# RWKV-6 with a channel MLP on one core: w, k and r of rounds 3 to 7 turned by VectorE from runs of steps, and the first level taken from loads one step back

## The chip, the cores and the metric

One core of a Trainium2 chip. The time is that of one execution on the device, in microseconds; the figure of a kernel is the median of its runs. Shares of busy time and single instructions come from one profiled execution.

## The reference

The first block is a linear recurrence over 768 steps, for 4 batches and 8 heads of 48 channels; the second a normalization and a two-layer MLP with a residual.

```python
for t in range(S):
    cur = einsum('bhd,bhe->bhde', u[None] * kt, vt)
    y[:, :, t] = einsum('bhd,bhde->bhe', rt, state + cur)
    state = wt[:, :, :, None] * state + einsum('bhd,bhe->bhde', kt, vt)
...
x = y.transpose(0, 2, 1, 3).reshape(B, S, H * D)
xn = (x - mu) / np.sqrt(var + 1e-06) * g_ln
out = x + np.maximum(xn @ w_ch1, 0.0) @ w_ch2        # 384 -> 1536 -> 384
```

Everything is float32.

## The kernel before, in words

**Units, rounds and levels.** The work is cut into eight rounds, numbered from 0, one for each batch and half of the sequence (384 steps). A round has two units of four heads. In a unit the 384 steps are six chunks of 64 steps, for each of two pairs of heads. Inside a chunk the weights from step s to step t (r at t times the decays between times k at s) are built in six levels: at level 0 for steps one apart, at level 1 for blocks of 2, and so on to blocks of 32. At each level PE multiplies k and r of all chunks (`quads`, result `a_ps`), then VectorE multiplies the later half of each block of r and of k by the block's decay product (`grow`, tile `rkT`), and copies the level's blocks under a mask into the matrix A (`keep`; at level 0 it is an AND with `bits`). PE needs the grown `rkT` for the next level.

**What feeds a round.** w, k and r of the next round are loaded with the steps on the partitions (`load`, tiles `nat_w`, `nat_k`, `nat_r`, one of each for an even and an odd unit), three transfers of 128 steps for each tensor and unit. PE turns them to channels on the partitions with an identity (`turned`: three transposes of 128x128 to a PSUM tile `w_ps`, `k_ps` or `r_ps`), and ScalarE copies them to SBUF: 36 transposes and 12 copies a round. This is done while the round before runs, at its levels 1 (w of both units), 2 (k and r of the first) and 3 (of the second); in round 2 at levels 3, 4 and 5. GpSimd (POOL) builds the products of decays over blocks (`totals`, tile `tot`, the last one `decay`). The term of the step itself, r times u times k summed over channels, comes from the untransposed tiles: `own_products` on POOL (tile `rk`), `own_sums` on VectorE (tile `own`), and times v in `own_term` on POOL (tile `vo`).

**What ends a round.** At levels 0 and 1 of the next round `states` runs for the two units of the old one (PE's `kv`, then ten dependent steps on VectorE, tile `s`), at levels 2 and 3 `outputs` (PE's `y`, to which VectorE adds `vo`, tile `x`). At level 5 `ends` turns k back (`kn_ps`).

**The MLP.** The MLP of a finished round is a list of 24 steps of three matmuls each (twelve for `h_ps`, twelve for `o_ps`). `fill(until, tasks)` puts them between the tasks of a level, so that PE has work while VectorE grows the next level; the table `UNTIL` says how many steps lie behind each level. From round 4 on it is four steps a level, in round 3 three. The tasks of a level are spread evenly over its MLP steps. A float32 matmul is two instructions on PE, so three matmuls read as x6 in the trace.

**Order.** PE, ScalarE, VectorE and POOL run in the order in which the program is written (`InOrder`, lines 39 to 48). Nearly all transfers are issued by SP, one queue in order: behind a transfer that waits for a buffer all later ones wait. The pool `p4` has four buffers a tag; its tag `raw` holds raw MLP weights early in the program. Every call goes through one helper, so that line 49 stands for all of them and the tiles tell them apart.

Lines: `load` 122, `turned` 306, `totals` 340, `own_products` 358, `own_sums` 369, `own_term` 401, `quads` 411, `grow` 431, `keep` 448, `states` 504, `outputs` 560, `mlp` 635, `fill` 692, the loop over rounds and levels from 821.

Of the kernel before, what the change touches and what calls it, by code (L numbers as in the profile page):

```python
# [9 lines left out]
F32 = mybir.dt.float32  # L10
# [42 lines left out]
def kernel(  # L53
# [79 lines left out]
    def load_rows(nm, q, eng):  # L133

        b, f, g = units[q]
        src = {"w": w, "k": k, "r": r}[nm]
        eng.dma_start(
            out=flat(nm, q)[:, 0 : NH * TT * D].rearrange("p (h x) -> p h x", h=NH),
            in_=src[b, ts(g, NH), ds(f * RN, RN)].rearrange("h (p c) d -> p h (c d)", c=TT),
        )  # L140

    def load_v(q, eng=SP):
# [161 lines left out]
    st, carry = {}, {}  # L304

    def turned(q, nm, pr):
        a = st.setdefault(q, {})
        if pr == 0:
            if nm == "w":
                if q % U == 0:  # L310
                    st["w"] = p1.tile([P, U, W], F32, tag="w", name=f"wT{q // U}")
                a["w"] = st["w"][:, q % U]
            elif "rk" not in a:

                rk = a["rk"] = p4.tile([P, 2, W], F32, tag="rkT", name=f"rkT{q}")
                a["r"], a["k"] = rk[:, 0], rk[:, 1]
        ps = ps_t.tile([P, RN], F32, tag="t", name=f"{nm}_ps{q}_{pr}")
# [40 lines left out]
    def own_products(q, eng):  # L358
        b, f, g = units[q]
        rk = st[q]["ruk"] = p1.tile([P, TT, NH, D], F32, tag="rk", name=f"rk{q}")  # L360
        eng.tensor_tensor(
            out=rk, in0=nat["k"][q % 2][..., 0:D], in1=nat["r"][q % 2][..., 0:D], op=ALU.mult
        )
        eng.tensor_tensor(
            out=rk, in0=rk,
            in1=u_bc[:, ts(g, NH)][:, None].broadcast_to([P, TT, NH, D]), op=ALU.mult,
        )

    def own_sums(q):
        o = st[q]["own"] = p4.tile([P, TT, NH], F32, tag="own", name=f"own{q}")  # L370
        DVE.tensor_reduce(out=o, in_=st[q]["ruk"], axis=AX.X, op=ALU.add)

    def products(q, eng=DVE):
# [27 lines left out]
    def own_term(q, eng):  # L401
        a = st[q]
        a["vo"] = p4.tile([P, TT, NH, D], F32, tag="vo", name=f"vo{q}")
        eng.tensor_tensor(
            out=a["vo"], in0=vn[q],
            in1=a["own"][:, :, :, None].broadcast_to([P, TT, NH, D]), op=ALU.mult,
        )

    a_ps = {}
# [38 lines left out]
    def keep(rnd, lev):  # L448
        n = 1 << lev
        A, ps = a_bufs[rnd % 2], a_ps[rnd]  # L450
        if lev == NLEV - 1:
# [268 lines left out]
    def units_of(rnd):  # L720
        return [U * rnd + g for g in range(U)] if rnd < NR else []

    def take(eng, q):

# [96 lines left out]
    for rnd in range(1, NR + 1):  # L821
# [3 lines left out]
        for lev in range(NLEV):  # L825
            slot = (rnd - 1) * NLEV + lev
            if rnd == 2:

                for q in old if lev < 2 else []:
                    (states, outputs)[lev](q)  # L830
                if lev < 2:
                    mlp_step()
            elif old and lev < 2 * U:
# [3 lines left out]
            for q in now:  # L837
                if slot:
                    quads(q, lev)
# [8 lines left out]
            if rnd == 1:  # L848
# [10 lines left out]
                if lev == 3:  # L859
                    tasks += each(load_vx, now, [SPO])  # L860
                if lev == 1:
                    tasks += each(product_sums, now)
                if lev in (4, 5):
                    own_term(now[lev - 4], POOL)
            if rnd == 2 and lev == 0:
                tasks += each(load_v, now) + each(load, new, "w")
            if rnd == 2 and lev == 2:
# [3 lines left out]
            if rnd == 2 and lev in (3, 4):  # L871
                tasks += each(own_term, now[lev - 3 :][:1], [POOL])
            if rnd > 2 and lev < 2:
                tasks += each(load, new, ["w", "kr"][lev])
            first = 3 if rnd == 2 else 1
            if rnd > 1 and new and first <= lev < first + 3:
                m = lev - first
                tasks += each(turned, new[m - 1 : m], "kr", pairs) if m else each(
                    turned, new, "w", pairs
                )  # L880
            if rnd == 2:
# [8 lines left out]
            if lev == 3 and rnd > 1:  # L890
                for q in now:
                    load_vx(q)
                for q in new:
                    load_v(q)
                if rnd > 2:
                    moments(rnd - 1)
                    tasks += each(norm, [rnd - 1])
            if lev == 4 and rnd > 2:
                tasks += each(turned_x, [rnd - 1], range(KC))
                tasks += each(own_products, new[:1], [POOL])  # L900
            if lev == NLEV - 1:

                if now:
                    mlp_step()
                if rnd > 2 and new:
                    own_sums(new[0])
                if rnd == 2:
                    tasks += each(own_products, new[:1], [POOL]) + each(own_sums, new[:1])
                if rnd >= 2:
                    tasks += each(own_term, new[:1], [POOL])  # L910
                    tasks += each(own_products, new[1:], [POOL])
                    tasks += each(own_sums, new[1:]) + each(own_term, new[1:], [POOL])
# [9 lines left out]
            if rnd == 1 and lev < NLEV - 1:  # L922

                n = (1, 2, 2, 1, 0, 0)[lev] * NP
                tasks += mixed([begin] * BEGINS[lev], [join] * JOINS[lev], ahead[:n])
                del ahead[:n]
# [35 lines left out]
```

## Time and profile before

| | |
|---|---|
| median of 11 runs | 586.73 us (584.99 to 590.91) |
| the profiled execution | 589.29 us, of it 587.5 from the first instruction to the last |
| PE busy | 574.9 us |
| VectorE (DVE) busy | 272.2 us |
| ScalarE (ACT) busy | 194.0 us |
| GpSimd (POOL) busy | 91.7 us |
| mean granted clock of TensorE | 0.985 |
| bytes moved | 36.52 MB, 62 GB/s |

A row of a timeline has the start, the length, the engine, the operation with out<-in, and, in brackets, how long the engine sat idle before it and what released it. A row of a group has the count, the busy time and the mean of one in ns, then the idle time before. For PE the mean of one overlaps with the next, so what PE steps cost is read from the start of one row to the start of another.

### The profile page before, as it was taken

The page shows a single profiled execution, that of the slowest core. Times are in us where ns is not written, and L with a number is a line of the kernel's source. Part 1 is how long each engine was busy: PE and PEld are TensorE (multiplying, and loading weights), DVE is VectorE, ACT ScalarE, POOL GpSimd, SP SyncE. Part 2 cuts the span into 40 slices and gives each one's busy share as a digit, 9 for nine tenths or more (in the row PEclk, how much of TensorE's full clock was granted, in tenths as well). Part 3 has the DMA queues.
Part 4 walks back from the last instruction along what each step waited for, and adds up shares of the span by engine and source line. Part 5 has one row for each costly group of instructions (what it writes and reads, how often), then busy time and mean ns, then how long its engine had stood idle before and what let it go on. Part 6 is the DMA issues. An engine that isn't in the chain of part 4 may idle for free.

```text
span 587.5 us, 19053 instructions
## 1 busy us (share of the span) xinstructions
PE 574.9 (98%) x8558; PEld 385.9 (66%) x8558; DVE 272.2 (46%) x576; ACT 194.0 (33%) x423; POOL 91.7 (16%) x124
## 2 busy tenths in 40 slices
PE   8999999999999999999999999999999999999997
PEld 6876765666666666676666666666666665666554
DVE  5788888777255443434362443336244441130000
ACT  3567597402452225212423115412241015202200
POOL 6130010204250026000530008000330000000000
PEclk9789799999999999999999999999999999999999
DMA  9938696046214402340204302021000000000000
GB/s 230 207 95 161 151 239 153 2 92 134 52 36 81 91 16 41 63 87 25 56 3 87 71 29 42 1 53 40 15 2 2 16 28 2 2 15 27 0 15 27
DMA packets 114192, 36.52 MB, mean 62 GB/s; under 512 B 104768, under 2 KB 111040, under 8 KB 114112
## 3 DMA queue, kind: packets, MB, share of 16 engines
q1 hardware_dynamic: 112240, 34.72, 26.8%
q8 instruction: 67, 1.10, 0.8%
q10 hardware_dynamic: 1872, 0.59, 0.4%
q14 instruction: 13, 0.11, 0.1%
HBM read 28.51 MB, written 4.72 MB: 57 GB/s over the span
## 4 chain that ended last, share of the span: by engine, by line
PE 92%; DVE 3%; ACT 3%; issue 1%; DMA 1%; ACTq 0%; DVEq 0%
PE o_ps L49 32%; PE h_ps L49 31%; PE a_ps L49 12%; PE y L49 4%; PE k_ps L49 2%; PE kv L49 2%; PE r_ps L49 2%; PE w_ps L49 2%; PE kn_ps L49 2%; PE xT_ps L49 1%; DVE w_sb L49 1%; PE own_ps L49 1%; PE idle L49 1%; ACT rest L49 1%; DVE rkT L49 1%
## 5 line engine op out<-in xcount | busy, mean ns | idle before, releaser
L49 PE MATMUL o_ps<-w_sb,h 128*128 128x384 f32 x576 | 199.1, 490 | 1.0 <-ACT h L49 1.0
L49 PE MATMUL h_ps<-xT,w_sb 128*128 128x384 f32 x576 | 199.6, 494 | 0.0
L49 PEld LDWEIGHTS h_ps<-xT,w_sb 128*128 128x128 f32 x576 | 106.0, 192 | 63.3 <-issue 1.2
L49 PEld LDWEIGHTS o_ps<-w_sb,h 128*128 128x128 f32 x576 | 104.3, 190 | 62.4 <-ACT h L49 2.3
L49 DVE TENSOR_TENSOR rkT<-rkT,tot 128x768 f32<-128x768 f32 (+1 forms) x96 | 75.7, 829 | 41.9 <-issue 26.0
L49 ACT ACTIVATE h<-h_ps 128x384 f32<-128x384 f32 x96 | 46.9, 489 | 145.0 <-PE h_ps L49 144.9
L49 PEld LDWEIGHTS a_ps<-rkT 48*64 48x64 f32 x4608 | 74.0, 138 | 21.0 <-issue 14.0
L49 PE MATMUL a_ps<-rkT 48*64 48x32 f32 x4608 | 79.2, 222 | 0.1
L49 DVE TENSOR_TENSOR o<-o_ps,x 128x384 f32<-128x384 f32 x24 | 13.4, 556 | 121.9 <-PE o_ps L49 121.8
L49 POOL TENSOR_TENSOR vo<-v,own 128x576 f32<-128x576 f32 x16 | 19.0, 1190 | 289.8 <-DVE own L49 250.2
L49 DVE SCALAR_TENSOR_TENSOR s<-s,decay,kv 128x48 f32<-128x48 f32 x160 | 29.3, 257 | 33.9 <-PE kv L49 33.9
L49 DVE TENSOR_TENSOR x<-y,vo 128x288 f32<-128x288 f32 x32 | 13.1, 452 | 54.5 <-PE y L49 54.5
L49 DVE COPY_PREDICATED A<-mask,a_ps 128x768 f32<-128x768 int8 x32 | 38.3, 1196 | 0.0
L49 ACT COPY rkT<-k_ps 128x384 f32<-128x384 f32 x31 | 13.9, 478 | 57.3 <-PE k_ps L49 57.1
L49 ACT ACTIVATE xT<-xT_ps,g_sb 128x384 f32<-128x384 f32 x24 | 13.6, 580 | 54.0 <-PE xT_ps L49 54.0
L49 ACT COPY rkT<-r_ps 128x384 f32<-128x384 f32 x31 | 14.2, 478 | 25.9 <-PE r_ps L49 25.9
L49 DVE TENSOR_SCALAR w_sb<-w_sb 128x384 f32<-128x384 f32 (+1 forms) x48 | 19.4, 405 | 0.8
L49 PE MATMUL r_ps<-ident,nat_r 128*128 128x128 f32 x108 | 16.7, 285 | 2.4 <-ACT rkT L49 1.6
L49 ACT COPY wT<-w_ps 128x384 f32<-128x384 f32 x31 | 13.9, 478 | 14.5 <-PE w_ps L49 14.4
L49 ACT ACTIVATE rstd<-mv,eps 128x3 f32<-128x3 f32 x8 | 2.4, 296 | 49.2 <-DVE mv L49 49.1
L49 DVE TENSOR_REDUCE own<-rk 128x12 f32<-128x576 f32 x12 | 9.0, 750 | 20.7 <-POOL rk L49 20.6
L49 PEld LDWEIGHTS r_ps<-ident,nat_r 128*128 128x128 f32 x108 | 13.0, 142 | 8.0 <-issue 2.5
(76 smaller groups left out, 524.5 us busy)
## 6 DMA issues: line engine op xcount, KB each, us to landing
raw<-in_moe_w_ch_dram SPq DMA_DIRECT2D x24, 384.0 KB, 4.1
v<-in_v_dram SPq DMA_DIRECT2D x48, 96.0 KB, 3.1
out_dram<-o SPq DMA_DIRECT2D x24, 192.0 KB, 1.9
nat_w<-in_w_dram SPq DMA_DIRECT2D x42, 96.0 KB, 3.1
nat_r<-in_r_dram SPq DMA_DIRECT2D x42, 96.0 KB, 2.8
nat_k<-in_k_dram SPq DMA_DIRECT2D x42, 96.0 KB, 2.9
vx<-v SPq DMA_DIRECT2D x28, 72.0 KB, 2.4
nat_r<-in_r_dram ACTq DMA_DIRECT2D x2, 288.0 KB, 5.0
```

The source lines that it names most:

```text
L49: return lambda *args, **kw: self.tc.keep_in_program_order(f(*args, **kw))
```

## The change

**Turning.** From round 3 on (prepared in rounds 2 to 6) w, k and r are no longer turned by PE. For each unit, tensor and pair of heads `stage` loads a tile in which a partition holds 12 consecutive steps of one head, and `squares` turns it by one VectorE instruction of 12 squares of 32x32 into channels on partitions, in place of three PE transposes and a ScalarE copy. A square needs 32 channels at a time, so a head takes two groups of 32 partitions, the second shifted by 32 channels and reading into the next step beyond channel 48. A tile is thus four transfers of 32 partitions by 560 numbers (2240 bytes each, one run in memory), and a round has 48 of them. The tiles use the four `raw` buffers. Staging of a level's tiles is issued one level before their squares: the staging of k and r of the first unit waits for the squares of w, that of the second unit for those of the first.

**The first level.** From round 3 on `quads` and `keep` leave level 0 out. Its entries of A are set to zero once in each of the two A buffers. Instead k and v are loaded a second time, one step back (`load_before`, into the `nat_w` tiles, which are free now), and the own term gets a second part: r times the k of the step before, summed over channels, kept at odd steps only (`next`), times the v of the step before. This is one more POOL step in `own_products`, a reduction and a small multiplication in `own_sums`, and two more POOL steps in `own_term`. k and r are still loaded with steps on partitions for these products. `grow` at level 0 stays. The two units of a round share the tiles one step back, so the second unit's load waits for the first unit's use.

**PE, levels 0 and 1 of round 4.** Before, from the states of an old unit at level 0 to the middle of level 1:

```order
L49 MATMUL kv_3310<-v_2259,kn_3244 64x48 x24
L49 MATMUL a_ps_0_3345<-rkT_2906 64x32 x24
L49 MATMUL a_ps_0_3345<-rkT_3058 64x32 x24
L49 MATMUL h_ps_0_4_3397<-xT_3150,w_sb 128x384 x3
L49 MATMUL h_ps_0_5_3406<-xT_3150,w_sb 128x384 x3
L49 MATMUL h_ps_0_6_3415<-xT_3150,w_sb 128x384 x3
L49 MATMUL h_ps_0_7_3424<-xT_3150,w_sb 128x384 x3
L49 MATMUL kv_3431<-v_2263,kn_3266 64x48 x24
L49 MATMUL a_ps_1_3466<-rkT_2906 64x32 x24
L49 MATMUL a_ps_1_3466<-rkT_3058 64x32 x24
L49 MATMUL h_ps_0_8_3527<-xT_3150,w_sb 128x384 x3
L49 MATMUL w_ps_0_3537<-ident,nat_w_88 128x128 x3
```

The same place on PE now:

```order
L49 MATMUL kv_3323<-v_2275,kn_3246 64x48 x24
L49 MATMUL h_ps_0_4_3371<-xT_3145,w_sb 128x384 x3
L49 MATMUL h_ps_0_5_3382<-xT_3145,w_sb 128x384 x3
L49 MATMUL h_ps_0_6_3393<-xT_3145,w_sb 128x384 x3
L49 MATMUL h_ps_0_7_3402<-xT_3145,w_sb 128x384 x3
L49 MATMUL kv_3409<-v_2279,kn_3270 64x48 x24
L49 MATMUL a_ps_1_3444<-rkT_2907 64x32 x24
L49 MATMUL a_ps_1_3444<-rkT_3078 64x32 x24
L49 MATMUL h_ps_0_8_3510<-xT_3145,w_sb 128x384 x3
L49 MATMUL h_ps_0_9_3519<-xT_3145,w_sb 128x384 x3
```

The level-0 products and the transposes are gone; MLP steps follow one another.

**VectorE, from level 5 to level 1 of the next round.** Before, from the two own sums of the coming round's units on (the second waits for POOL), then the old unit's states, level 0 and its mask, the other unit's states, level 1:

```order
L49 TENSOR_REDUCE own_4038<-rk_3968 128x12
L49 TENSOR_REDUCE own_4068<-rk_4053 128x12
L49 COPY s_4105<-kv_4106 128x48 x2
L49 SCALAR_TENSOR_TENSOR s_4105<-s_4105,decay_3297,kv_4106 128x48 x10
L49 TENSOR_TENSOR rkT_3686<-rkT_3686,wT_3536 128x2x384
L49 TENSOR_TENSOR rkT_3848<-rkT_3848,wT_3536 128x2x384
L49 TENSOR_TENSOR A_125<-a_ps_0_4143,bits_163 128x768
```

The same place on VectorE now:

```order
L49 TENSOR_REDUCE own_4015<-rk_3944 128x12
L49 TENSOR_REDUCE next_4017<-nat_w_88 128x12
L49 TENSOR_SCALAR next_4017<-next_4017,odd 128x12
L49 TENSOR_REDUCE own_4062<-rk_4053 128x12
L49 TENSOR_REDUCE next_4064<-nat_w_88 128x12
L49 TENSOR_SCALAR next_4064<-next_4064,odd 128x12
L49 COPY s_4099<-kv_4100 128x48 x2
L49 SCALAR_TENSOR_TENSOR s_4099<-s_4099,decay_3310,kv_4100 128x48 x10
L49 TENSOR_TENSOR rkT_3668<-rkT_3668,wT_3508 128x2x384
L49 TENSOR_TENSOR rkT_3849<-rkT_3849,wT_3508 128x2x384
```

The sums one step back stand before the states, and the masking of level 0 is gone. Four squares (`STREAM_TRANSPOSE`) follow the masks of levels 1 and 2 and the normalization at level 3.

**SP, around level 2.** Before, from the loads of the coming units' k, r and w on:

```order
L125 DMA nat_k_91<-in_k_dram 128x4x48 x3
L125 DMA nat_r_93<-in_r_dram 128x4x48 x3
L125 DMA nat_w_88<-in_w_dram 128x4x48 x3
L125 DMA nat_w_89<-in_w_dram 128x4x48 x3
L145 DMA v_4624<-in_v_dram 128x4x48 x3
```

SP now, after the loads of w's runs:

```order
L125 DMA nat_k_91<-in_k_dram 128x4x48 x3
L125 DMA nat_r_93<-in_r_dram 128x4x48 x3
L163 DMA k_runs_0_3525<-in_k_dram 32x560 x4
L163 DMA k_runs_1_3530<-in_k_dram 32x560 x4
L163 DMA r_runs_0_3535<-in_r_dram 32x560 x4
L163 DMA r_runs_1_3546<-in_r_dram 32x560 x4
L163 DMA k_runs_0_3676<-in_k_dram 32x560 x4
L163 DMA k_runs_1_3681<-in_k_dram 32x560 x4
L163 DMA r_runs_0_3689<-in_r_dram 32x560 x4
L163 DMA r_runs_1_3694<-in_r_dram 32x560 x4
L743 DMA out_dram<-o_0_0_3702 128x384
```

Thirty-two transfers of runs stand between the loads of k and r and the first output; each group of four waits for VectorE's squares to free its buffer.

**The diff**, cut to its core; `FIRST` is 3:

```diff
+    def stage(q, nm, pr, eng=SP):
...
+        t = p4.tile([P, WC, 2], F32, tag="raw", name=f"{nm}_runs{q}_{pr}")
+        t = staged[q, nm, pr] = t.rearrange("p n two -> p (n two)")[:, 0 : NS * D]
+        for j in range(2):
+            first = src.offset + ((b * H + g * NH + 2 * pr + j) * S + f * RN) * D
+            for e in range(HP // SQ):
...
+                eng.dma_start(
+                    out=t[ds(HP * j + SQ * e, SQ), 0:n],
+                    in_=bass.AP(
+                        tensor=src.tensor, offset=first + SQ * e, ap=[[NS * D, SQ], [1, n]]
+                    ),
+                )
+    def load_before(q, src, i, eng=SP):
...
+        for c in range(TT):
+            eng.dma_start(
+                out=nat["w"][i][:, c, :, 0:D],
...
+    def squares(q, nm, pr):
+        a = st[q] if pr else turned_to(q, nm)
+        DVE.transpose(
+            out=a[nm][:, ts(pr, RN)].rearrange("p (t s) -> p s t", s=NS),
+            in_=staged.pop((q, nm, pr)).rearrange("p (s d) -> p s d", s=NS)[..., 0:SQ],
+        )
@@ own_products
+        if q >= FIRST * U:
+            k1 = nat["w"][0][..., 0:D]
+            eng.tensor_tensor(out=k1, in0=k1, in1=nat["r"][q % 2][..., 0:D], op=ALU.mult)
@@ own_sums
+            DVE.tensor_reduce(out=o, in_=nat["w"][0][..., 0:D], axis=AX.X, op=ALU.add)
+            DVE.tensor_scalar(out=o, in0=o, scalar1=odd, scalar2=None, op0=ALU.mult)
@@ own_term
+            eng.tensor_tensor(out=a["vo"], in0=a["vo"], in1=v1, op=ALU.add)
@@ loop over rounds and levels
             for q in now:
-                if slot:
+                if slot and (lev or rnd < FIRST):
                     quads(q, lev)
...
-            if rnd > 1 and new and first <= lev < first + 3:
+            if rnd > 1 and new and first - 1 <= lev < first + 3:
                 m = lev - first
-                tasks += each(turned, new[m - 1 : m], "kr", pairs) if m else each(
-                    turned, new, "w", pairs
-                )
+                turns = [(new, "w"), (new[:1], "kr"), (new[1:], "kr")]
+                if m >= 0:
+                    tasks += each(squares, *turns[m], pairs)
+                if m < 2:
+                    tasks += each(stage, *turns[m + 1], pairs)
...
-                    tasks += each(norm, [rnd - 1])
+                    tasks = each(norm, [rnd - 1]) + tasks
...
                 if rnd >= 2:
+                    tasks += each(load_before, new[1:], [k], [0])
                     tasks += each(own_term, new[:1], [POOL])
+                    tasks += each(load_before, new[1:], [v], [1])
                     tasks += each(own_products, new[1:], [POOL])
```

Two smaller edits come with it: the own sums of round 1 on PE are mixed among the other tasks of their level, and round 2 places an MLP step between the outputs of its two old units as well as behind them.

85 lines of the change are left out of this document (64 added, 21 removed).

## Prediction

> **What bounds the kernel now.** I read the page's busy times first, then the chain that ended last, then busy times by stretch over the rounds that the change touches.
>
> ```profile
> span 587.5 us, 19053 instructions
> PE 574.9 (98%) x8558; PEld 385.9 (66%) x8558; DVE 272.2 (46%) x576; ACT 194.0 (33%) x423; POOL 91.7 (16%) x124
> PE 92%; DVE 3%; ACT 3%; issue 1%; DMA 1%; ACTq 0%; DVEq 0%
> 145.00:213.00 68.00, 66.75 (x1135) 45.70 (x1127) 31.98 (x64) 22.23 (x50) 12.09 (x12) 1.00 0.31 61
> 213.00:281.00 68.00, 68.00 (x1073) 45.75 (x1073) 27.77 (x58) 19.77 (x44) 12.80 (x12) 1.00 0.24 50
> 281.00:349.00 68.00, 68.00 (x1069) 45.83 (x1069) 28.42 (x63) 19.76 (x44) 13.20 (x12) 1.00 0.24 50
> 349.00:417.00 68.00, 68.00 (x1093) 45.84 (x1087) 27.94 (x59) 19.76 (x44) 12.96 (x12) 1.00 0.15 33
> ```
>
> The stretches give length, then busy time of PE, PE's weight loads, DVE, ACT and POOL, then clock, DMA share and GB/s. From 213 to 417 us PE never pauses, at full clock, while DVE is busy 28 of 68 us. PE time that goes there shortens the run one for one, unless another engine makes PE wait. So I need two things: what PE steps are worth from start to start, and how much room each new DVE step has before PE's next use of it.
>
> **What it removes from PE.** Times are read from start to start, since matmuls overlap and their busy times count the overlap twice. This is round 5 on PE, from level 0 (first three rows) to the end of level 1.
>
> ```profile
> 292.42 1.57 PE L49 MATMUL a_ps<-rkT 48*64 48x32 f32 x96
> 293.92 8.01 PE L49 MATMUL h_ps<-xT,w_sb 128*128 128x384 f32 x24
> 301.86 0.92 PE L49 MATMUL kv<-v,kn 64*64 64x48 f32 x48
> ...
> 304.09 2.20 PE L49 MATMUL h_ps<-xT,w_sb 128*128 128x384 f32 x6
> 306.13 0.49 PE L49 MATMUL w_ps<-ident,nat_w 128*128 128x128 f32 x3
> ...
> 308.39 0.82 PE L49 MATMUL w_ps<-ident,nat_w 128*128 128x128 f32 x6
> ...
> 310.99 0.49 PE L49 MATMUL w_ps<-ident,nat_w 128*128 128x128 f32 x3
> ...
> 313.35 0.25 PE L49 MATMUL y<-v,A 64*64 64x48 f32 x1
> ```
>
> The first-level products take 293.92 - 292.42 = 1.50 us. Four MLP steps alone take 301.86 - 293.92 = 7.94 us; four MLP steps with 12 transposes take 313.35 - 304.09 = 9.26 us, so 12 transposes are worth 1.32 us, 0.11 us each. A round has 36 of them, 3.95 us.
>
> - Transposes of five rounds: 5 x 3.95 = 19.8 us.
> - First-level products of rounds 3 to 7: 5 x 1.50 = 7.5 us.
>
> A regular round shrinks by 5.45 us. The Trainium skill (TensorE: Matmul & The Clock Gate, Part 4) gives a PE transpose about 275 ns in a kernel and 390 ns alone; by 275 ns the 180 transposes would be 49 us and the gain about 57 us, an estimate. The step of 0.11 us decides here: the latency shows only in the duration of one, not in the queue's advance.
>
> With the transposes goes a small wait for their PSUM copies in round 2:
>
> ```profile
> 158.32 0.55 PE L49 MATMUL k_ps<-ident,nat_k 128*128 128x128 f32 x3 [0.58 <-ACT rkT L49]
> 159.44 0.93 PE L49 MATMUL r_ps<-ident,nat_r 128*128 128x128 f32 x6 [0.19 <-ACT rkT L49]
> 160.55 0.55 PE L49 MATMUL kn_ps<-ident,rkT 128*128 128x128 f32 x3 [0.18 <-ACT rkT L49]
> ```
>
> That is 0.95 us. ACT also loses twelve copies a round, and is on no chain here.
>
> **What it adds to DVE: squares.** No 32x32 transpose stands in the trace. The nearest rows of 384 elements a lane or more:
>
> ```profile
> L49 DVE TENSOR_TENSOR o<-o_ps,x 128x384 f32<-128x384 f32 x24 | 13.4, 556 | 121.9 <-PE o_ps L49 121.8
> L49 DVE COPY_PREDICATED A<-mask,a_ps 128x768 f32<-128x768 int8 x32 | 38.3, 1196 | 0.0
> L49 POOL TENSOR_TENSOR vo<-v,own 128x576 f32<-128x576 f32 x16 | 19.0, 1190 | 289.8 <-DVE own L49 250.2
> ```
>
> I take 0.56 us (same size, one pass), with 1.2 us as the upper end and 0.4 below. Twelve a round are 6.7 us, plus two more reductions, less the 0.95 us masking of level 0: DVE goes from 28 of 67.8 us to about 36 of 62.4. What matters is where they stand:
>
> ```profile
> 178.39 1.87 DVE L49 COPY_PREDICATED A<-mask,a_ps 128x768 f32<-128x768 int8 x1
> 214.12 1.20 DVE L49 TENSOR_TENSOR rkT<-rkT,tot 128x384 f32<-128x384 f32 x2 [0.36 <-PE a_ps L49]
> 306.58 1.86 DVE L49 COPY_PREDICATED A<-mask,a_ps 128x768 f32<-128x768 int8 x1
> 335.64 1.26 DVE L49 TENSOR_SCALAR xn<-x,mv,rstd 128x384 f32<-128x384 f32 x3
> 349.74 2.14 DVE L49 TENSOR_TENSOR rkT<-rkT,tot 128x384 f32<-128x384 f32 x4 [0.36 <-PE a_ps L49]
> ```
>
> The tightest level is 3: xn ends at 336.90, and by 349.74 DVE owes level 4's two multiplications (1.83), its mask (about 1) and an output addition (0.56). With 1.32 us of PE time gone from between, 12.84 - 1.32 - 3.4 = 8.1 us is left for four squares: they cost nothing up to 2.0 us each. In round 3, whose levels are shorter, the room is some 4 us, 1.0 us each. Cover is thus there at 0.56; at 1.2 only round 3 pays, about 1 us.
>
> **What it adds to SP: the staging.** Per round 48 transfers of 32 rows replace six for w; six loads one step back come on top, k and r's own loads stay.
>
> ```profile
> 308.70 4.06 SPq L125 DMA_DIRECT2D nat_w<-in_w_dram  x6
> nat_w<-in_w_dram SPq DMA_DIRECT2D x42, 96.0 KB, 3.1
> L49 SPq DMA_DIRECT2D raw<-in_moe_w_ch_dram x24: 327/340/1241, 4.5 to 91.9; - x24
> ```
>
> A level's batch is 16 transfers. At raw's issue of 0.34 us and a landing of 3.1 us a batch takes 16 x 0.34 + 3.1 = 8.5 us; at nat_w's 0.68 us apiece, 14.0 us. I take 8.5: a transfer has 32 rows, and raw's 128 rows are the nearer. The four buffers make batch, squares, batch, squares a chain on DVE and SP: from the mask of level 1 to the multiplications of level 5 are 349.74 - 308.44 = 41.3 us, less 3.95 that PE saves, less 3.4, less two times four squares (4.5): 29.4, or 14.7 us a batch. In round 3 it is 214.12 - 180.26 = 33.9, so 11.0 us a batch. Both hold 8.5; at 14.0 round 3 alone pays 6 us. Batch w goes out a level ahead, with no squares before it.
>
> **What it adds between rounds.** Level 5 of round 5, level 0 of round 6; T counts from level 5's products on PE.
>
> ```profile
> 348.72 1.60 PE L49 MATMUL a_ps<-rkT 48*64 48x32 f32 x96
> 359.50 0.92 PE L49 MATMUL kv<-v,kn 64*64 64x48 f32 x48
> 351.80 0.75 DVE L49 TENSOR_REDUCE own<-rk 128x12 f32<-128x576 f32 x1
> 356.67 0.75 DVE L49 TENSOR_REDUCE own<-rk 128x12 f32<-128x576 f32 x1 [4.12 <-POOL rk L49]
> 360.49 1.84 DVE L49 SCALAR_TENSOR_TENSOR s<-s,decay,kv 128x48 f32<-128x48 f32 x10 [3.06 <-PE kv L49]
> 355.22 1.41 POOL L49 TENSOR_TENSOR rk<-rk,u_bc 128x576 f32<-128x576 f32 x1
> 358.61 1.47 POOL L49 TENSOR_TENSOR tot<-wT 128x768 f32<-128x768 f32 x1
> 362.25 1.82 DVE L49 TENSOR_TENSOR rkT<-rkT,wT 128x768 f32<-128x768 f32 x2
> 355.17 1.49 SPq L125 DMA_DIRECT2D nat_k<-in_k_dram  x3
> ```
>
> DVE's second own sum already waits 4.12 us for POOL, and queued behind it are the states and level 0's multiplications. New order: own sum ends T = 3.8, next sum and its mask of odd steps 4.7; POOL own term 1.2 + 1.2 + 1.4, ending 7.6; the second unit's products 3 x 1.45, ending 11.9; DVE's next sum to 12.8, states 1.84, multiplications 1.82, ending 16.5. PE wants these for level 1 at 10.8 + 0.7 + 7.9 + 0.7 = 20.2, since no level 0 stands before it now: 3.7 us of room. Two-input steps of DVE and POOL can hold each other:
>
> ```profile
> 168.21 3.39 DVE L49 TENSOR_TENSOR rkT<-rkT,wT 128x768 f32<-128x768 f32 x2
> 168.79 2.00 POOL L49 TENSOR_TENSOR rk<-rk,u_bc 128x576 f32<-128x576 f32 x1
> ```
>
> Here two multiplications took 3.39 instead of 1.82, so 2.1 us is left. The second unit's load one step back starts after the first unit's next sum, T = 4.7, issues for 1.5, lands 3.1 later, 9.3; POOL wants it at 10.5. The decay totals start at 15.5, first one done at 17.0; DVE wants it at about 22. All hidden. In round 2 the last squares fall into this very level, 2.2 us and a wait for their batch of perhaps 2, against 2.1 to 3.7: 0 to 2 us late. With round 3's shorter levels I take 2 us of new waits, bounds 0 and 10.
>
> **The sum.** The profiled run took 589.29 us (span 587.5). 589.3 - 19.8 - 7.5 - 0.95 + 2.0 = 563.0. That run lies 2.56 us above the median of 586.73; the median goes to 586.7 - 26.2 = **560.5 us**, own range 557 to 565.
>
> **The rivals.** (a) The level boundary becomes late: POOL's longer chain, the load in it and port conflicts eat the 2.1 us and 2 us more, every round. For it: 4.12 us of waiting there today, and three more POOL steps a unit. Against: 3.7 us of room by durations. Price 5 x 2 = 10 us: 570.5.
>
> (b) Slower: the staging is the bound. Place: levels 1 to 3, SP and the four buffers. It decides where a batch passes 14.7 us; each microsecond more costs PE 2 a round, and at 17.4 us, about 0.9 us a transfer beyond the landing, the 5.45 us are gone. With 1.0 us each a batch is 19.1, 2 x 4.4 = 8.8 us a round, and 44 us over five: 604.5. For it: nat_w's 0.68 us apiece with larger transfers. Against: nat_w's transfers go out 0.68 us apart in sixes and still land after a median of 3.1 us; one after another the sixth would land after 6 x 3.1 - 3.4 = 15. They overlap. The Trainium skill (DMA: Bandwidth & Descriptors, Rules for kernel authors) advises against splitting a load over parts of the partitions, since the parts serialize, and puts some 2.0 us of fixed cost on a DMA; by that a batch would be 32 us, an estimate. The row's landings disagree with that reading.
>
> (c) The squares are slow, 2 us or more each: level 3 fills, and each 0.1 us above costs 0.4 us a round. At 2.4 us that is 8 us in the regular rounds and more in round 3: 573. Nothing but the absence of a row is for it.
>
> (d) That PE waits elsewhere and nothing is gained is excluded by the three stretches with PE busy 68.00 of 68.00.
>
> **How the numbers follow.** Forecast 0.66; (a) 0.20; (b) 0.05; (c) 0.04; better than 557, through shorter tails behind small matmuls, 0.05. The range 556.5 to 573 leaves out (b), part of (a) and (c), and a little below. A difference under 0.3% (1.8 us) cannot be told from none. Faster 0.92 (all but (b) and the tails of (a) and (c)), same 0.02, slower 0.06.
>
> **What would show it.** Right: PE still without pauses from 213 us on; a regular round of about 62.4 us instead of 67.8; squares near 0.56 us; staging landed before its squares on DVE; level 0's multiplications done before PE's level 1. Wrong: PE idle before a_ps released by DVE, growing each round ((a) if at level 1, (b) or (c) if at levels 4 and 5); DVE idle before a square, released by a DMA (b).

## The result, and the profile after

The changed kernel takes **565.74 us** (median of 12 runs, 563.67 to 568.25) where the kernel before takes 586.95 us beside it: ratio 0.9639, 95% interval 0.9619 to 0.9658. That is 21.2 us faster; the forecast was 26.2 us faster, 560.5 us. The profiled execution of the changed kernel took 565.91 us. One run of an experiment, `r2_early`, took 1107.25 us in a slower state and is left out of that kernel's figures.

First the page: span, busy times, and the chain that ended last by engine.

```profile
span 564.2 us, 18202 instructions
PE 547.8 (97%) x7898; PEld 359.2 (64%) x7898; DVE 333.1 (59%) x654; ACT 168.9 (30%) x363; POOL 133.7 (24%) x157
PE 82%; DVE 7%; ACT 4%; SPq 2%; issue 2%; DMA 1%; POOL 1%; DVEq 0%; POOLq 0%; ACTq 0%
```

PE is busy 27.1 us less (574.9 before), while its pauses grew from 587.5 - 574.9 = 12.6 to 16.4 us. Its share of the chain fell from 92% to 82%. Where the pauses are, the stretches show (length, busy time of PE, its weight loads, DVE, ACT and POOL, then clock, DMA share, GB/s):

```profile
145.00:205.00 60.00, 55.58 (x889) 35.91 (x888) 46.91 (x87) 13.38 (x29) 19.57 (x18) 0.97 0.64 146
205.00:270.00 65.00, 65.00 (x949) 41.91 (x949) 41.33 (x77) 14.74 (x32) 22.34 (x19) 1.00 0.53 118
270.00:330.00 60.00, 60.00 (x910) 39.42 (x911) 40.83 (x77) 14.75 (x32) 21.35 (x18) 1.00 0.56 126
330.00:395.00 65.00, 65.00 (x941) 41.83 (x939) 40.32 (x73) 14.75 (x32) 21.07 (x21) 1.00 0.53 117
```

From 205 to 395 us PE never pauses. The loss is in round 2 and its boundary to round 3, where the first staged round is prepared. PE's waits there, with the pause and what ended it in brackets:

```profile
137.57 4.14 PE L49 MATMUL h_ps<-xT,w_sb 128*128 128x384 f32 x12 [1.36 <-DVE o L49]
...
149.17 1.60 PE L49 MATMUL a_ps<-rkT 48*64 48x32 f32 x96
...
153.60 0.88 PE L49 MATMUL kn_ps<-ident,rkT 128*128 128x128 f32 x6 [0.69 <-DVE rkT L49]
...
169.76 0.90 PE L49 MATMUL a_ps<-rkT 48*64 48x32 f32 x48 [2.28 <-DVE rkT L49]
171.81 1.05 PE L49 MATMUL a_ps<-rkT 48*64 48x32 f32 x48 [1.15 <-DVE rkT L49]
172.79 7.56 PE L49 MATMUL o_ps<-w_sb,h 128*128 128x384 f32 x18
```

The row at 149.17 has no wait; it is the products of level 5, from which the boundary is counted. All waits but the first end with DVE's `rkT`, so the question goes to DVE, then to POOL and SP, for which DVE waited:

```profile
149.32 0.86 DVE L49 STREAM_TRANSPOSE rkT<-k_runs 128x384 f32<-128x384 f32 x1 [1.13 <-DMA k_runs<-in_k_dram]
150.48 0.86 DVE L49 STREAM_TRANSPOSE rkT<-r_runs 128x384 f32<-128x384 f32 x1 [0.30 <-DMA r_runs<-in_r_dram]
152.30 0.85 DVE L49 STREAM_TRANSPOSE rkT<-r_runs 128x384 f32<-128x384 f32 x1 [0.96 <-DMA r_runs<-in_r_dram]
...
161.00 0.87 DVE L49 STREAM_TRANSPOSE rkT<-r_runs 128x384 f32<-128x384 f32 x1 [2.00 <-DMA r_runs<-in_r_dram]
...
164.98 0.75 DVE L49 TENSOR_REDUCE next<-nat_w 128x12 f32<-128x576 f32 x1 [1.71 <-POOL nat_w L49]
...
167.99 3.77 DVE L49 TENSOR_TENSOR rkT<-rkT,wT 128x768 f32<-128x768 f32 x2
```

```profile
155.67 1.15 POOL L49 TENSOR_TENSOR vo<-v,own 128x576 f32<-128x576 f32 x1 [11.81 <-DVE own L49]
...
163.54 1.41 POOL L49 TENSOR_TENSOR nat_w<-nat_w,nat_r 128x576 f32<-128x576 f32 x1 [1.05 <-DMA nat_w<-in_k_dram]
```

```profile
150.78 3.62 SPq L163 DMA_DIRECT2D k_runs<-in_k_dram  x8
154.50 4.96 SPq L163 DMA_DIRECT2D r_runs<-in_r_dram  x8
159.55 1.50 SPq L174 DMA_DIRECT2D nat_w<-in_k_dram  x3
```

DVE waits 4.39 us for staged runs. It does so ahead of the first unit's own sums too, and POOL, which waits for these, starts its chain late. On SP the second unit's load one step back stands behind the last batch and goes out only at 159.55; POOL waits 1.05 us for it, DVE's `next` waits for POOL, and level 0's multiplications end at 171.76, after PE has run out of work.

A regular boundary, round 4 to 5, for comparison (DVE, POOL, PE):

```profile
280.57 0.75 DVE L49 TENSOR_REDUCE own<-rk 128x12 f32<-128x576 f32 x1 [5.61 <-POOL rk L49]
...
284.97 3.77 DVE L49 TENSOR_TENSOR rkT<-rkT,wT 128x768 f32<-128x768 f32 x2
```

```profile
273.78 1.15 POOL L49 TENSOR_TENSOR vo<-v,own 128x576 f32<-128x576 f32 x1 [6.06 <-DVE own L49]
```

```profile
269.88 1.60 PE L49 MATMUL a_ps<-rkT 48*64 48x32 f32 x96
...
290.18 1.57 PE L49 MATMUL a_ps<-rkT 48*64 48x32 f32 x96
...
332.45 1.60 PE L49 MATMUL a_ps<-rkT 48*64 48x32 f32 x96
```

The multiplications end at 288.74, the second unit's last. PE takes the first unit's at 290.18 and the second's one half (0.75 us) later, so the room is 290.93 - 288.74 = 2.2 us.

Counted from level 5's products on PE, level 0's multiplications begin after 284.97 - 269.88 = 15.1 us here and after 167.99 - 149.17 = 18.8 at the end of round 2, 3.7 later. Of that, 2.6 us are there when POOL begins the first unit's own term (after 3.9 us here, 6.5 there), and 1.05 is the wait for the load one step back. PE on its side is done with its other work after 20.3 us here and after 18.3 there (169.76 - 2.28 - 149.17). 2.2 - 3.7 - 2.0 = -3.5 us: these are PE's waits of 2.28 and 1.15.

The regular round lasts 332.45 - 269.88 = 62.57 us.

The squares, as a group and at level 3 of the same round:

```profile
L49 DVE STREAM_TRANSPOSE rkT<-r_runs 128x384 f32<-128x384 f32 x20 | 15.6, 837 | 3.3 <-DMA r_runs<-in_r_dram 3.3
259.00 1.54 DVE L49 STREAM_TRANSPOSE rkT<-k_runs 128x384 f32<-128x384 f32 x2
...
262.23 1.79 DVE L49 TENSOR_TENSOR rkT<-rkT,tot 128x768 f32<-128x768 f32 x2
```

One takes 0.84 us alone and 15.6 / 20 = 0.78 us in line; level 4's multiplications end at 264.02, 5.9 us ahead of PE's products at 269.88.

### The profile page after: what moved, and what is told of

Same layout as the page of the kernel before. It is cut to its first block, busy times and chain, and to the rows that moved or that the text cites. A ratio compares the mean times of both kernels' runs of the same rounds, so it can differ in the third digit from the quotient of the medians.

```text
span 564.2 us, 18202 instructions
## 1 busy us (share of the span) xinstructions
PE 547.8 (97%) x7898; PEld 359.2 (64%) x7898; DVE 333.1 (59%) x654; ACT 168.9 (30%) x363; POOL 133.7 (24%) x157
## 4 chain that ended last, share of the span: by engine, by line
PE 82%; DVE 7%; ACT 4%; SPq 2%; issue 2%; DMA 1%; POOL 1%; DVEq 0%; POOLq 0%; ACTq 0%
PE o_ps L49 33%; PE h_ps L49 27%; PE a_ps L49 9%; PE y L49 4%; PE kv L49 2%; DVE rkT L49 2%; DVE w_sb L49 2%; ACT rest L49 2%; PE kn_ps L49 2%; SPq L163 1%; PE xT_ps L49 1%; PE own_ps L49 1%; PE k_ps L49 1%; PE idle L49 1%; PE r_ps L49 1%
## 5 line engine op out<-in xcount | busy, mean ns | idle before, releaser
L49 PE MATMUL h_ps<-xT,w_sb 128*128 128x384 f32 x576 | 196.4, 491 | 2.5 <-DVE o L49 1.4
L49 PEld LDWEIGHTS o_ps<-w_sb,h 128*128 128x128 f32 x576 | 106.1, 191 | 67.2 <-ACT h L49 2.3
L49 DVE TENSOR_TENSOR rkT<-rkT,tot 128x768 f32<-128x768 f32 (+1 forms) x96 | 78.6, 860 | 30.7 <-issue 17.6
L49 PEld LDWEIGHTS a_ps<-rkT 48*64 48x64 f32 x4128 | 66.8, 138 | 24.7 <-issue 13.1
L49 PE MATMUL a_ps<-rkT 48*64 48x32 f32 x4128 | 71.8, 223 | 3.9 <-DVE rkT L49 3.9
L49 DVE SCALAR_TENSOR_TENSOR s<-s,decay,kv 128x48 f32<-128x48 f32 x160 | 29.3, 257 | 18.9 <-PE kv L49 18.9
L49 POOL TENSOR_TENSOR nat_w<-nat_w,nat_r 128x576 f32<-128x576 f32 x10 | 14.8, 1477 | 101.3 <-DMA nat_w<-in_v_dram 67.5
L49 DVE TENSOR_TENSOR rkT<-rkT,wT 128x768 f32<-128x768 f32 x16 | 24.9, 1594 | 0.9 <-PE a_ps L49 0.8
L49 DVE TENSOR_SCALAR w_sb<-w_sb 128x384 f32<-128x384 f32 (+1 forms) x48 | 19.4, 405 | 0.8
L49 PEld LDWEIGHTS y<-v,A 64*64 64x64 f32 x384 | 12.7, 134 | 7.6 <-issue 4.4
L49 DVE STREAM_TRANSPOSE rkT<-r_runs 128x384 f32<-128x384 f32 x20 | 15.6, 837 | 3.3 <-DMA r_runs<-in_r_dram 3.3
L49 POOL TENSOR_TENSOR tot<-wT 128x768 f32<-128x768 f32 x6 | 12.4, 2073 | 20.2 <-DVE rkT L49 20.2
```

What stands on the lines that cost most here:

```text
L49: return lambda *args, **kw: self.tc.keep_in_program_order(f(*args, **kw))
```

## The experiments

Theory A: the missing 5 us is lost in round 2 alone. B: it is lost in all rounds. C: POOL's longer chain at the level boundary makes PE wait.

**1. The two halves of the change apart.** `squares_only` turns by squares, but keeps level 0 on PE and has no load one step back:

```diff
-                if slot and (lev or rnd < FIRST):
+                if slot:
                     quads(q, lev)
...
-        if lev == 0 and rnd >= FIRST:
+        if False:
```

> The turning by squares alone: level 0 is multiplied on PE as before, no loads one step back and no terms from them. Theory A (the staging of round 2 starts too late): 586.9 - 19.8 - 0.95 + about 2 of waits around 150 to 170 us = 568 us. Theory C (the longer POOL chain of the first level is what makes PE wait): no waits left, 566.2 us.

Measured: 567.77 us (566.1 to 569.2), ratio 0.967 (0.9634 to 0.9706), 19.4 us under the kernel before. The median is nearer to theory A's 568 than to C's 566.2, but the interval holds both. The profile speaks for A: from 145 to 205 us PE is busy 58.17 of 60 us, so 1.8 us of waits are left, where A has about 2 and C none; the change has 4.4. `level0_only` keeps PE's transposes and w, k and r's old loads, and takes level 0 from loads one step back in buffers of their own:

```diff
-            if rnd > 2 and lev == 1:
-                tasks += each(load, new, ["kr"])
+            if rnd > 2 and lev < 2:
+                tasks += each(load, new, ["w", "kr"][lev])
...
-                tasks += each(squares, *turns[m], pairs)
+                tasks += each(turned, new[m - 1 : m], "kr", pairs) if m else each(
+                    turned, new, "w", pairs
+                )
```

> The first level alone: w, k and r are still turned by PE; the loads one step back go into the four raw buffers, so the second unit's load does not wait for the first unit's use. Removed PE work 7.5 us. Theory A: 586.9 - 7.5 = 579.4, with waits of 1 us at most: 579 to 580.5. Theory C (POOL's longer chain makes PE wait at level 1): 2 us a round back, 586 to 590 at worst, at least 583.

Measured: 586.2 us (584.64 to 589.31), ratio 0.9987 (0.9962 to 1.0012): nothing, though PE has 7.5 us less to do. The time is one that theory C forecast, but the pauses are not where C has them: PE waits 7.4 us at `r_ps` for ACT (1.6 before) and 0.4 at `a_ps` for DVE. In a regular round, ACT's order (two rows) and PE's pause:

```profile
262.92 0.30 ACT L49 ACTIVATE rstd<-mv,eps 128x3 f32<-128x3 f32 x1 [10.39 <-DVE mv L49]
263.12 0.84 ACT L49 COPY rkT<-k_ps 128x384 f32<-128x384 f32 x2
```

```profile
263.63 0.55 PE L49 MATMUL r_ps<-ident,nat_r 128*128 128x128 f32 x3 [1.73 <-ACT rkT L49]
```

The change also moves `norm` ahead of the level's other tasks. With transposes still on PE, the copies of `k_ps` then stand behind `rstd`, which waits for DVE's `mv`. `level0_norm` puts that one line back:

```diff
-                    tasks = each(norm, [rnd - 1]) + tasks
+                    tasks += each(norm, [rnd - 1])
```

> The kernel with the first level alone, as in level0_only, and one line put back as it stood before the change: norm (whose square root ACT computes) is issued behind the copies of the turned k and r again, not ahead of them. In level0_only TensorE waited 1.73 us a round at r_ps, 7.4 us in all (1.6 before): ACT's rstd waits for VectorE's mv until 262.92, and the copies of k_ps stand behind it on ACT. Theory queue: that order alone ate the gain; the waits at r_ps fall back to about 1.6 us, and of the 7.5 us of removed products about 6 to 7 are seen: 580 to 581 us beside 587 for the kernel before, ratio 0.987 to 0.989. Rival transfers: the pause is the later loading of k and r (POOL's longer chain frees their buffers late), and stays: 586 us, ratio 0.998.

Measured: 578.33 us (578.01 to 580.69), ratio 0.985 (0.9816 to 0.9885), 8.8 us under; PE's waits at `r_ps` for ACT are down to 0.8 us, as theory queue had it. ACT now copies first:

```profile
257.43 0.86 ACT L49 COPY rkT<-k_ps 128x384 f32<-128x384 f32 x2 [7.20 <-PE k_ps L49]
...
260.85 0.30 ACT L49 ACTIVATE rstd<-mv,eps 128x3 f32<-128x3 f32 x1
```

One task's place in ACT's queue had eaten the whole gain of level 0; in the change as made it costs nothing, since no copies are left behind it. The parts sum to 19.4 + 8.8 = 28.2 us; together they bring 21.2. So by the medians some 7 us, with about 3 either way by the intervals, are lost only when both are done; a part of that is the clock (last section). By the profiles it is less: against the 12.6 us of the kernel before, PE's pauses are 564.4 - 550.1 = 14.3 us with the squares alone, 576.3 - 564.9 = 11.4 with level 0 alone, and 16.4 with both, so that 3.3 us of pauses come only with both.

**2. Round 2.** `r2_early` stages and turns one level earlier there:

```diff
-            first = 3 if rnd == 2 else 1
+            first = 2 if rnd == 2 else 1
```

> Staging and squares of round 3's tiles begin one level earlier in round 2 (levels 2 to 4 instead of 3 to 5); nothing else changes. Theory A: the missing 5 us are PE waits at one place only, the end of round 2, where the staging starts too late and its tail, the load one step back behind it on SP and POOL's chain end in the level-0 multiplications (2.28 + 1.15 + 0.69 us of PE waits at 153 to 172 us). Those go, about -4 us, but w's squares (2.9 us) now stand on DVE ahead of the output addition that PE already waits for (1.36 us at 137.6), which gives up to 2.9 back: 564.5 us, 563 to 566, with the wait at 137 us grown to about 4 and those at 153 to 172 gone. Rival B: the loss is spread (more DMA traffic, longer chains in every round): the waits at 153 to 172 stay and the time is 565.7 plus what the later output addition costs, 566 to 568.

Measured: 568.14 us (567.53 to 572.84), ratio 0.9692 (0.9648 to 0.9736), no better than the change, and not theory A's 563 to 566. The wait only moved:

```profile
157.93 2.42 PE L49 MATMUL kn_ps<-ident,rkT 128*128 128x128 f32 x9 [4.54 <-DVE rkT L49]
```

Now DVE does round 2's own products and sums (5.4 us) and the squares of w at the same level, and it still waits 5.0 us in all for staged runs of k and r. `r2_early_pool` gives those products to POOL, one level earlier:

```diff
-            if rnd == 2 and lev == 2:
-                for q in now:
-                    take(DVE, q)
-                    tasks += each(load, new[q % U :][:1], "kr")
+            if rnd == 2 and lev < 2:
+                own_products(now[lev], POOL)
+            if rnd == 2 and lev in (1, 2):
+                own_sums(now[lev - 1])
+                tasks += each(load, new[lev - 1 :][:1], "kr")
```

> As r2_early, and round 2's own products are made by POOL one level earlier in place of DVE, which takes about 3 us of DVE work from ahead of that output addition. Theory A: both waits go, 565.7 - 4 - 1 = 561 us (559.5 to 562.5), 26 us under the kernel before as the removed PE work says. Rival B: 565.7 as after the change (564.5 to 567).

Measured: 566.12 us (563.75 to 567.65), ratio 0.9634 (0.9599 to 0.967), as the change and as rival B has it; theory A had 561. PE's wait for `o` is gone, but 2.8 us remain at `kn_ps` (its waits, with total, count and longest):

```profile
PE kn_ps L49 <- DVE rkT L49: 2.8, 1, 2.8
```

`r2_first1_pool` goes one level further (`first = 1` in all rounds):

> Round 2 stages and turns at the same levels as every later round (w at level 1, k and r at 2 and 3; the change has 3, 4 and 5), and its own products are made by GpSimd at levels 0 and 1, as in r2_early_pool. Theory staging: what is left in round 2 (2.8 us of waits at kn_ps in r2_early_pool, and 1.2 at a_ps) comes from VectorE waiting 4.6 us for the second batch, which is issued from 142.0 to 151.1; a level earlier it lands about 10 us sooner and the waits at kn_ps go: 562 to 564 us, against 565.7 for the change as made. Rival boundary: the first-level chain over GpSimd (rk, nat_w, next, then the 3.8 us grow) and the lower clock after a pause decide there, so that the time stays at 565 to 567.

Measured: 564.9 us (562.05 to 568.42), ratio 0.9617 (0.9579 to 0.9654), between the theory and its rival. `kn_ps` no longer waits for DVE; the pause is now at `xT_ps`, where DVE squares w ahead of the statistics (DVE, then PE):

```profile
123.92 2.91 DVE L49 STREAM_TRANSPOSE wT<-w_runs 128x384 f32<-128x384 f32 x4
126.68 1.41 DVE L49 BATCH_NORM_STATS2 stats<-x 128x6 f32<-128x384 f32 x3
```

```profile
129.42 1.44 PE L49 MATMUL xT_ps<-ident,xn 128*128 128x128 f32 x6 [2.70 <-DVE xn L49]
```

`r2_norm_first` turns that order round; `r2_norm_again` is the same kernel:

```diff
-                    tasks += [lambda: moments(1), lambda: norm(1)]
+                    tasks = [lambda: moments(1), lambda: norm(1)] + tasks
```

> r2_first1_pool with one order changed: at level 1 of round 2 the statistics and norm of round 1 (VectorE, ACT) stand ahead of the squares of w, not behind them. In r2_first1_pool TensorE waited 2.70 us at xT_ps for VectorE's xn, since own's sum (0.72 us) and four squares (2.91 us) ran before BATCH_NORM_STATS2, and the granted clock of the next 10 us was 0.69 and 0.97. Theory queue: the wait at xT_ps goes and with it the low clock behind it: 564.9 - 2.7 - 1.7 = 560.5 us, 5 us under the change as made. Rival: the 2.9 us of squares now delay the next grow by as much, and TensorE waits at a_ps or kn_ps in place of xT_ps: 564 to 566 us.

> The same kernel as r2_norm_first, measured once more: its first interval (0.9548 to 0.962) touches that of the changed kernel (0.9619 to 0.9658). Theory (the change lost 5 to 6 us in round 2, and this order gets most of it back): ratio to the kernel before 0.956 to 0.960 again, 561 to 563 us beside 587. Rival (the first measurement was a lucky one): ratio 0.962 to 0.965.

Measured: 562.09 us (561.02 to 564.98), ratio 0.9584 (0.9548 to 0.962), and 563.88 us (562.02 to 565.09), ratio 0.9601 (0.9576 to 0.9626): less of a gain than theory queue's 560.5, and the second time above the 561 to 563 that were expected. The stretch that had 55.58 of 60 us, in `r2_norm_first`:

```profile
145.00:205.00 60.00, 58.82 (x995) 38.51 (x994) 48.15 (x87) 13.37 (x29) 21.98 (x18) 1.00 0.58 128
```

PE's pauses are down to 559.3 - 546.09 = 13.2 us, 3.2 less than in the change. The medians lie 3.7 and 1.9 us under it; each interval still touches its interval, and the granted clock of these runs was a little higher (medians of 0.994 and 0.991, against 0.9895), so that this is the fastest of all is likely and not settled. A holds in its place (round 2), but not in its cause: no single step is late there. The squares, the own products, the statistics and the staged loads all meet on DVE and SP in one round, and each step that was moved uncovered the next.

**3. The rooms that the prediction counted on.** `squares_twice` turns every square twice into the same place (`for _ in range(2): DVE.transpose(...)`):

> The changed kernel with every square of the staged loads turned twice into the same place: four more STREAM_TRANSPOSE of 0.74 us, 3.0 us, at each of three levels of a round. Theory room: in the regular rounds grow at level 4 ends at 264.0 and TensorE takes its result at 269.9, so 3.0 us more are hidden there and nothing is paid; only round 2, where VectorE is late already at levels 4 and 5, pays 3 to 6 us: 569 to 572 us, and from 205 to 395 us TensorE stays at 65.00 of 65. Rival (the squares bound every round): 3.0 us in each of five rounds, 15 us, 580 us, with pauses at a_ps or o_ps in every round.

Measured: 570.78 us (568.84 to 572.11), ratio 0.9711 (0.9675 to 0.9746), about 5 us over the change, as theory room has it, and in a regular stretch PE never pauses with 7.4 us more on DVE:

```profile
270.00:330.00 60.00, 60.00 (x908) 39.04 (x907) 48.23 (x86) 14.09 (x31) 21.87 (x18) 1.00 0.55 121
```

The price of a square is hidden there; round 2 pays (from 145 to 205 us PE is busy 52.38 of 60 us, 55.58 in the change). `pool_more2` makes the second unit's product of k and r three times on POOL (`for _ in range(3 if q >= FIRST * U and q % U else 1)`):

> The changed kernel with the product of k and r of the second unit made three times by GpSimd from round 3's units on: 2 x 1.41 us, 2.8 us, more at the level boundary, in front of own, next and the first grow. Theory boundary: grow 0 ends at 288.74 and TensorE takes it at 290.18, a room of 1.4 us, so each of the four regular boundaries pays 1.4 us and the one from round 2 to 3, which is late already, 2.8 us: 8.5 us, 574 us, and TensorE's waits at a_ps <- DVE rkT show 1.4 us a round. Rival: GpSimd is not on that path (the time stays at 566); other rival: no room at all, 5 x 2.8 = 14 us, 580 us.

Measured: 572.13 us (571.06 to 574.51), ratio 0.9742 (0.9705 to 0.9778). Every regular boundary now has one pause:

```profile
270.00:330.00 60.00, 59.29 (x889) 38.31 (x890) 36.11 (x73) 13.88 (x31) 24.79 (x20) 1.00 0.54 122
297.63 0.90 PE L49 MATMUL a_ps<-rkT 48*64 48x32 f32 x48 [0.71 <-DVE rkT L49]
```

Some 3.0 us more on POOL (4.39 us for three, 1.41 for one) cost 0.7: the room is 2.3 us, as read above, and POOL is on that path. (The expected 1.4 us a round counted the room to the first unit's products.) The four regular pauses make 2.8 of the 6.4 us; the others are lost around round 2, where PE now waits 4.16 us at the boundary and 1.98 at `kn_ps`. C is thus no loss in the regular rounds, only a room that is nearly used. `halves` splits each staging transfer into two of 16 partitions:

```diff
-                eng.dma_start(
-                    out=t[ds(HP * j + SQ * e, SQ), 0:n],
+                for z in range(2):
+                    eng.dma_start(
+                        out=t[ds(HP * j + SQ * e + 16 * z, 16), 0:n],
```

> The changed kernel with each staging transfer of 32 partitions split into two of 16: 96 a round instead of 48, the same bytes. Theory issue: SP's issue of a transfer takes about 0.46 us whatever its size, so a batch of 32 takes 14.7 us, and 16.7 with the landing, against the 14 us between two levels; each of three batches is 2.7 us late, 8 us a round in four regular rounds, and more in round 2, where SP is late already: 600 to 615 us, with VectorE's squares waiting for DMA in every round. Rival bytes: what a batch takes is set by its bytes, not by its count; 566 us as before. Rival room: SP stays off the path in the regular rounds (its loads are early enough) and only round 2 pays: 568 to 575 us.

Measured: 637.18 us (634.53 to 639.59), ratio 1.0871 (1.0815 to 1.0926). A stretch, two rows of SP, and the group of the squares of r:

```profile
205.00:270.00 65.00, 55.40 (x787) 36.29 (x778) 37.09 (x70) 14.74 (x32) 17.80 (x16) 0.89 0.47 98
217.60 8.49 SPq L164 DMA_DIRECT2D k_runs<-in_k_dram  x16
226.19 7.31 SPq L164 DMA_DIRECT2D r_runs<-in_r_dram  x16
L49 DVE STREAM_TRANSPOSE rkT<-r_runs 128x384 f32<-128x384 f32 x20 | 17.1, 855 | 58.6 <-DMA r_runs<-in_r_dram 49.9 <-DMA k_runs<-in_k_dram 8.7
```

A batch is 15.8 us of issue: a transfer has half the bytes and still takes 0.46 to 0.53 us. The theory of the issue holds in kind, but the price is 71 us and not 30 to 50. PE's pauses grew to 632.8 - 571.28 = 61.5 us, 45 more, about what was expected in all; the other 23.5 us are in PE's busy time (571.28 against 547.75), at a mean granted clock of 0.938 (0.988 in the change). The expectation had no term for the clock.

**4. The clock behind a pause.** In the changed kernel the 18 `o_ps` matmuls at 172.79 took 7.56 us, after PE had paused 2.28 and 1.15 us (columns: busy time of PE, clock, DMA share, GB/s):

```profile
165.00:170.00 5.00, 2.72 (x71) 1.00 0.60 156
170.00:175.00 5.00, 3.85 (x99) 0.74 0.56 119
175.00:180.00 5.00, 5.00 (x16) 0.92 0.96 172
```

`warm_2to3` puts matmuls of zeros into these two pauses:

```diff
+                if rnd == FIRST and lev == 1:
+                    warm(12 if q == now[0] else 6, "t")
```

> The changed kernel with six matmuls of zeros put on TensorE into the two waits between rounds 2 and 3: four (about 1.4 us) ahead of the first a_ps group of round 3, where it waited 2.28 us, and two (about 0.7 us) ahead of the second, where it waited 1.15 us. They add no time to the path if they fit into the waits. Theory clock: the granted clock after the pause (0.74 from 170 to 175 us, 0.92 from 175 to 180) is a result of the pause; with the pause filled it stays at 1.00 there, the 18 o_ps matmuls behind it take 6.1 us and not 7.6, and the time is 1.5 to 1.7 us less: 564.0 us. Rival: the clock falls for another reason (the work before the pause), or zeros don't hold it: 565.7 us, 18 o_ps in 7.6 us.

The same place in its profile:

```profile
165.81 2.86 PE L49 MATMUL idle<-nought 128*128 128x384 f32 x8
168.61 0.90 PE L49 MATMUL a_ps<-rkT 48*64 48x32 f32 x48
169.44 1.56 PE L49 MATMUL idle<-nought 128*128 128x384 f32 x4
170.93 0.90 PE L49 MATMUL a_ps<-rkT 48*64 48x32 f32 x48
171.76 6.07 PE L49 MATMUL o_ps<-w_sb,h 128*128 128x384 f32 x18
```

The 18 matmuls take 6.07 us, at clock 1.00: with the pauses filled the clock stayed. One profile could show that by chance, but others agree: with a pause of 4.16 us at this place (`pool_more2`) the clock is 0.66, 0.50 and 0.81 from 170 to 185 us, and in the five profiles of experiment 2 and in `squares_twice`, whose waits there are 1.15 us or less, it is 1.00 from 165 to 185. So the low clock here was very likely a result of the pauses. The time is 565.45 us (563.4 to 566.35), ratio 0.9631 (0.9597 to 0.9666): the 1.5 us did not show. The filling was mis-sized, 2.86 + 1.56 = 4.4 us instead of 2.1 (six matmuls are the twelve instructions in the rows), against 3.4 us of pauses; it gives some of it back. What is left is below what these runs can tell.

## Why the prediction was right or wrong

**What bounds the kernel.** Right. PE paces it, and PE's busy time came down by 27.1 us where 27.3 was counted. That the two meet so closely is in part luck: a regular round shrank by 67.82 - 62.57 = 5.25 us (from 280.90 to 348.72 before) where 5.45 was counted, 26.2 in five rounds, and the rest of the 27.1 is likely the clock (below).

**Removed work.** Right in size: the squares alone brought 19.4 us (17.3 to 21.5) where 20.75 of transposes and their waits were counted, level 0 alone 8.8 (6.8 to 10.8) for 7.5. The step of 0.11 us a transpose held, not a duration of 275 ns: a regular round is 62.57 us, forecast 62.4.

**Squares.** 0.56 us was too low, 0.78 was measured, inside the bounds. In regular rounds that costs nothing, as said (`squares_twice`).

**Staging.** The batch was forecast at 8.5 us; the last one of round 2 took 159.46 - 150.78 = 8.7 us to issue and about 2 more to land, 10.8. The issue was put too low (0.34 us a transfer, measured 0.45 to 0.62), the landing too high (3.1, measured 2.0 to 2.1). In a regular round a batch has 14.7 us and in round 3 11.0, and neither makes PE wait; in round 3 that left almost nothing. For round 2, which prepares the first staged round, the prediction worked out no such room. There SP issues both batches of k and r without a break from 142.86 to 159.46, the first as soon as the squares of w free its buffers, and DVE waited 4.39 us.

**The level boundary.** PE's need was placed at T = 20.2 and measured at 290.18 - 269.88 = 20.3; the multiplications were to end at 16.5, or 18.1 with the port conflict, and end at 18.9. The room after the conflict was put at 2.1; counted in the same way, to the first unit's products, it is 1.4. That `pool_more2` finds 2.3 is the second unit's later place on PE, which the prediction left out: the two errors nearly cancel, and the good agreement is luck. Rival (a) did not come: no regular boundary is late. The one from round 2 to 3 is.

**New waits, 2 us: the step that failed.** The prediction said that squares and a wait for their batch at the end of round 2 come "0 to 2 us late". PE's pauses grew by 3.8 us in all, 4.75 if the 0.95 of removed waits are added back; inside the bounds of 0 to 10, but more than twice the size. What was not counted: DVE waits for staged runs already ahead of level 5's multiplications and the first unit's own sums, so that POOL's chain starts 2.6 us late. The load one step back stands behind the last batch on SP, 1.05 us more. PE comes to the boundary 2.0 us earlier than in a regular round; the prediction named the shorter levels, but gave them no size. And in the middle of round 2 PE now waits 1.36 us for `o`, which stands on DVE behind that round's own products. The low clock behind the pauses cost another 1.5 us on the `o_ps` matmuls. No run moved the load alone; the shares of 2.6 and 1.05 are read from the trace.

**From the profile to the median.** The pauses explain 2.8 of the 5.2 us between 560.5 and 565.7: they grew by 3.8 us where 2.0 - 0.95 = 1.05 was forecast. The other 2.4 are in the step that took the profile's saving for the median's: the profiled run of before had a granted clock of 0.985 and lay 2.56 us above its median, that of the change 0.988 and 0.17 above. The spans differ by 23.3 us, the medians by 21.2. Some of PE's 27.1 us is likely clock and not work: by the slope in the last section 0.003 of clock is 1.3 us.

Rivals (b) and (c) did not come either, but `halves` shows that (b) was a real danger: at 15.8 us of issue and some 2 of landing a batch is past (b)'s 17.4 us, and the kernel is 50 us slower than before, more than the 2 us a round that (b) put on each microsecond would give.

## What to carry to other kernels

A steady round that has room says nothing of the round that first feeds it: cost the transition by itself, with every queue in which the new work stands ahead of old work. Taking work off the bounding engine is worth its full size only if the tasks in the other engines' queues are put in order for it; one `norm` ahead of two copies was worth the whole of level 0. And a pause of the matmul engine can cost more than its length, by the low clock that may follow.

## What the runs showed of the hardware

- **The granted clock falls after pauses shorter than expected, and not only after pauses.** A pause of 2.70 us (`r2_first1_pool`), or 2.28 and 1.15 us close together, was followed by stretches of 5 us at a mean of 0.69 to 0.97. All pauses from 2.28 us up, in all runs, were followed by a low clock; below 2 us some were (1.61 us in `squares_twice`: 0.87 and 0.78) and some were not (1.36 us at 137.57, four of 1.73 us in `level0_only`). The Trainium skill (TensorE: Matmul & The Clock Gate, HAM oscillation — how this bites in real kernels) puts the limit at gaps of about 3.4 us; here shorter ones were enough. Nor is a pause needed: in the kernel before PE was busy without a break from 55 to 75 us, and the clock was 0.82 from 60 to 65 and 0.50 from 65 to 70. Why is open.
- **It goes with much of the scatter between runs.** Over the 47 runs of the kernel before that were timed beside the experiments, the granted clock was 0.982 to 0.999, and the span fell with it (correlation -0.93, some 0.42 us for each 0.001). The parts in experiment 1 ran at a median of 0.994, the change at 0.9895, the kernel before at 0.988; corrected by that slope the parts give 17 and 6 us, the change 21, and the loss of doing both is nearer 3 than 7 us, as the pauses say too. The correction takes all of the clock for chance; what of it a kernel's own pauses cause, it removes wrongly.
- **A transfer's issue price did not shrink with its size:** 0.46 and 0.53 us on SP for 35 KB, 0.45 and 0.62 for 70 KB in the rows shown, and about 2 us to land for both. The Trainium skill (DMA: Bandwidth & Descriptors, Rules for kernel authors) advises against splitting a load over partitions; `halves` agrees in kind, while the landings overlap, so that 16 transfers take about 10 us and not the 32 that the prediction worked out from that page.
- **DVE and POOL hold each other in two-input steps:** level 0's two multiplications took 3.77 us beside POOL's products and totals at both boundaries shown. Before, they took 3.39 us once beside POOL's products, and 1.82 at 362.25, where POOL had only a `decay` of 128x24 to do; that one took 1.73 us instead of 0.23.
